# Segment rows and left q and k moved from GpSimd's DMA queue to SyncE's and ScalarE's

## The chip, the cores and the metric

The kernel runs on one core of one Trainium2 chip. Its metric is the time of one execution on the device, in microseconds (us). Before the change the median of three runs is 1866.62 us (1864.03 to 1872.82).

## The reference, cut to what matters

```python
x = A_x                                   # 2048 rows x 1024, bf16
xn = layernorm(x)
return x + A(xn, mem0, Wq, Wk, Wv, Wo, 32) + B(xn, w_r, w_gate, w_up, w_down)

def A(x, mem0, Wq, Wk, Wv, Wo, seg_len):  # 32 heads of 128, 8 memory rows
    mem = mem0
    for s in range(64):                   # segments of 32 rows
        h = concat([mem, x[32 * s:32 * s + 32]])       # 40 rows
        q, k, v = h @ Wq, h @ Wk, h @ Wv               # per head
        o = softmax(mask(q @ k.T * 128 ** -0.5)) @ v @ Wo
        mem = o[:8]                       # the next segment's memory
        outs.append(o[8:])
    return concat(outs)
```

`B` chooses two of the 2048 rows by a router, puts them through a gated MLP of width 3584 and adds the results to those rows. The memory makes the 64 segments a chain: each needs the one before.

## The kernel before, in words

**Rows.** Of a segment's 32 input rows the first 24 go with its 8 memory rows through the loop over segments, 32 rows at a time. The last 8 rows of a segment don't depend on anything but x in q, k and v; these "left" rows are taken for four segments together (a group: 32 left rows), and their q and k are stored to DRAM (`ql_d`) one group ahead. In the code `s` is the segment, `G` its group and `j` its place in the group (0 to 3; I call them first to fourth).

**Weights.** Wq, Wk, Wv and Wo are cut into 64 granules of 512 KB, numbered 0 to 63. 44 stay in SBUF; 20 are streamed from DRAM in each segment (`STREAMED`: 2, 5, 6, 9, 13, 17, 21, 25, 29, 33, 36, 39, 42, 45, 47, 50, 53, 56, 59, 62). From the second segment on granule 6 and half of 25 come from PSUM, so 19 loads a segment remain, `g<-wsc` at line 366, one of them of 256 KB. They go through five buffers ("slots"). "Load 39" is the load of granule 39. `fetch` is called after a granule's use and loads the one four places on; the load waits for TensorE to be done with the slot, which held the granule five places back.

**A segment.** Phases 0 to 5 project q, k and v, two halves each, from eight granules each (line 817); attention runs between them; phase 6 is the projection with Wo (line 586); at the end VectorE adds the result to the rows (line 885), and the 8 memory rows are turned into the next segment's input. `hook(p, kc, fn)` calls `fn` after granule `kc` of phase `p`. Each engine does its instructions in the order in which this program writes them; a queue's instruction that waits holds all behind it.

**Transfers.** SyncE (SP) issues the weight loads. GpSimd issues `load_seg` (four transfers of 24 rows x 256 columns, for the next segment, at hook (2, 4)), the four stores of a segment's output at its end, `new_lx` (left q and k of this segment, from `ql_d`, at granule 9 of phase 6), and the left rows' loads and stores. ScalarE issues the stores to `ql_d` (line 628): of a group's four, one at the start of phase 1 in the second segment, one at the start of phase 2 in the third, and one at the end of phase 5 in each of the two.

**Semaphores.** Each transfer has a completion semaphore. GpSimd's transfers share eight of them (`DMASW0` to `DMASW7`); SP's and ScalarE's share another eight (`DMAHW0` to `DMAHW7`), given out in turn over both engines. A transfer that gets a semaphore waits, on the engine that issues it, until the transfer that had it last has landed.

`X[s % 2]` holds a segment's rows: loaded, then scaled in place (`norm_seg`, line 294), then the sum with the output (`OB`), which is stored from it. A load of segment s + 1 therefore waits for the stores of segment s - 1.

Of the kernel before, what the change touches and what calls it, by code (L numbers as in the profile page):

```python
# [50 lines left out]
def kernel(  # L51
# [16 lines left out]
    nc = tc.nc  # L68
# [4 lines left out]
    SEG = int(A_seg_len)  # L73
# [9 lines left out]
    XM = SEG - M  # L83
# [3 lines left out]
    x2 = A_x[0]  # L87
    out2 = out[0]
# [37 lines left out]
    ql_d = [dram.tile([4, P, 512], BF16, name=f"ql_d{t}") for t in range(NT)]  # L126
# [25 lines left out]
    X = [const.tile([P, 256], BF16, name=f"X{b}") for b in range(2)]  # L152
# [46 lines left out]
    for s in range(4):  # L199
        nc.vector.tensor_copy(out=SELM[:, s, :, 0:XM],  # L200
                              in_=IDENT[:, 32 * s:32 * s + XM].unsqueeze(1).to_broadcast([P, 4, XM]))
        nc.vector.tensor_copy(out=SELL[:, s, :, :],
                              in_=IDENT.rearrange("p (s c) -> p s c", c=32)[:, :, XM:SEG])
        nc.vector.tensor_copy(out=SELR[:, s, :, :],
                              in_=IDENT.rearrange("p (s c) -> p c s", c=32)[:, XM:SEG, :])
# [67 lines left out]
    def two_rows(m, tag):  # L273
        t = one.tile([P, 4], F32, tag=tag, name="RI")
        nc.vector.tensor_copy(out=t[:, 0:1], in_=m[:, 0:1])
        nc.vector.reciprocal(out=t[:, 1:2], in_=m[:, 1:2])
        return t

    def load_seg(s):
        for g in range(4):  # L280
            nc.gpsimd.dma_start(out=X[s % 2][32 * g:32 * g + XM, :],  # L281
                                in_=x2[s * SEG:s * SEG + XM, 256 * g:256 * (g + 1)])

    def norm_seg(s):

        x = X[s % 2]
        mr = two_rows(MR[:, s, :], "ri")
        ab = mr[:, 2:4]
        nc.vector.tensor_scalar(out=ab[:, 0:1], in0=mr[:, 1:2], scalar1=1.0, scalar2=KMSK, op0=ALU.add, op1=ALU.mult)
        nc.vector.tensor_scalar(out=ab[:, 1:2], in0=mr[:, 0:1], scalar1=mr[:, 1:2], scalar2=-1.0, op0=ALU.mult, op1=ALU.mult)  # L290
        xn = front.tile([P, 256], BF16, tag="st", name="XN")
        nc.vector.tensor_scalar(out=xn[:, :], in0=x[:, :], scalar1=mr[:, 0:1], scalar2=mr[:, 1:2],
                                op0=ALU.subtract, op1=ALU.mult)
        nc.vector.tensor_scalar(out=x[:, :], in0=x[:, :], scalar1=ab[:, 0:1], scalar2=ab[:, 1:2],
                                op0=ALU.mult, op1=ALU.add)
        return xn
# [8 lines left out]
    def gview(st):  # L305
        return st.rearrange("p (g c) r -> p c g r", c=2)

    def turn_rows(xn, xl):

        return turn(xn), turn(xl, 1) if xl is not None else None  # L310

    def new_st(turned):
        PTx, PTl = turned
        st = front.tile([P, KC, SEG], BF16, tag="st", name="ST")
        nc.scalar.copy(out=gview(st)[:, :, :, 0:XM], in_=PTx[:, :, :, 0:XM])
        if PTl is None:
            return st, None
        stl = one.tile([P, KC, SEG], BF16, tag="stl", name="STL")
        nc.scalar.copy(out=gview(stl), in_=PTl[:, :, :, :])
        return st, stl  # L320

    def mem_to_st(OB, st):
        PTm = turn(OB)
        nc.vector.tensor_copy(out=gview(st)[:, :, :, XM:SEG], in_=PTm[:, :, :, XM:SEG])
# [11 lines left out]
    def norm_left(t, G):  # L336
        mr = two_rows(MLR[:, G, :], "ri")
        nc.vector.tensor_scalar(out=t[:, :], in0=t[:, :], scalar1=mr[:, 0:1], scalar2=mr[:, 1:2],
                                op0=ALU.subtract, op1=ALU.mult)

    def sum_left(t, G):

        mr = two_rows(ML[:, G, :], "ri")
        nc.vector.tensor_scalar(out=mr[:, 0:1], in0=mr[:, 0:1], scalar1=mr[:, 1:2], scalar2=-1.0,
                                op0=ALU.mult, op1=ALU.mult)
        nc.vector.tensor_scalar(out=mr[:, 1:2], in0=mr[:, 1:2], scalar1=1.0, scalar2=None, op0=ALU.add)
        nc.vector.tensor_scalar(out=t[:, :], in0=t[:, :], scalar1=mr[:, 1:2], scalar2=mr[:, 0:1],
                                op0=ALU.mult, op1=ALU.add)
# [20 lines left out]
    def part(t, jq):  # L369
        return t[jq][:, :] if isinstance(t, list) else t[:, 512 * jq:512 * (jq + 1)]  # L370
# [16 lines left out]
    def bring_back(c, copy):  # L387
        back[c] = one.tile([P, 512], BF16, tag=(roles[0], "bE", "kt", "bC")[c], name="BK")
        copy(out=back[c][:, :], in_=KEPT_COLS[KEPT_WHOLE][c])  # L389

    def kept_piece(g, c, copy):
        t = [t for q, t in queued if q == g][0]
        copy(out=t[:, 512 * c:512 * (c + 1)], in_=KEPT_COLS[g][c])  # L393
# [38 lines left out]
    load_x(0)  # L432
    nc.sync.dma_start(out=WRB, in_=B_w_r.unsqueeze(0).to_broadcast([P, D]))
    load_seg(0)
    XL0 = load_left(0, one.tile([P, 256], BF16, tag="vl0", name="XL0")[:, :])
    OB = one.tile([P, 256], BF16, tag="bA", name="MEM0")
# [21 lines left out]
    norm_left(XL0, 0)  # L458
    ST, STL = new_st(turn_rows(norm_seg(0), XL0))
    mem_to_st(OB, ST)  # L460

# [30 lines left out]
    def new_lx(s):  # L492
        t = lx[0] = one.tile([P, 512], BF16, tag="bA", name="LX")
        G, j = divmod(s, 4)
        nc.gpsimd.dma_start(out=t[:, :], in_=ql_d[G].rearrange("m (x s) c -> (m x) s c", s=4)[:, j])  # L495

    lx = [None]

# [60 lines left out]
        return out  # L559

    after_first = []

    def begin(u):
        PS = psL.tile([P, 512], F32, tag="accl", name="WL" if u == "o" else "PSl")
        units[u] = [PS, 16 if u == "o" else 8]
# [66 lines left out]
    for s in range(NSEG):  # L632
        G, j = divmod(s, 4)
# [9 lines left out]
        def hook(p, kc, fn):  # L643
            hooks.setdefault((p, kc), []).append(fn)
# [128 lines left out]
        def run_passes(p, kc):  # L773

            for u, g in passes.pop((p, kc), []):
                if g == 8 * p + kc or p >= 7:
                    t = res_tiles[g] if p >= 7 else held[g]
                else:
                    t = held.get(g) or res_tiles[g]
                one_pass(u, g, t)  # L780
# [7 lines left out]
            hook(2, 3, lambda: sum_left(xl_of[0], G - 1))  # L788
        hook(*((1, 0) if s > 0 else (2, 3)), clear_pl)
        if s > 0:  # L790
            hook(0, 0, lambda: bring_back(3, nc.scalar.copy))
            hook(0, 1, lambda: bring_back(0, nc.vector.tensor_copy))
            hook(2, 1, lambda: kept_piece(KEPT_PART, 2, nc.vector.tensor_copy))
            hook(2, 2, lambda: kept_piece(KEPT_PART, 3, nc.vector.tensor_copy))
# [1 line left out]
        hook(3, 4, exponent)  # L796
        hook(3, 4, lambda: soften(0))
        if s + 1 < NSEG:
            hook(2, 4, lambda: load_seg(s + 1))
        if j == 0 and G + 1 < NT:  # L800
            hook(4 if s == 0 else 1, 1, get_left)
            hook(5, 3, lambda: norm_left(nxt["xl"], G + 1))
# [6 lines left out]
        for p, (mat, half) in enumerate(PHASES):  # L809
# [3 lines left out]
            for kc in range(KC):  # L813
                g = 8 * p + kc
                Gv = back if s > 0 and g == KEPT_WHOLE else granule(g)
                for jq in range(4):
                    nc.tensor.matmul(PSm[32 * jq:32 * jq + 32, :], lhsT=ST[:, kc, :], rhs=part(Gv, jq),  # L817
                                     start=(kc == 0), stop=(kc == KC - 1), tile_position=(0, 32 * jq))
# [45 lines left out]
        for w in range(16):  # L864
            if w == 5:
                attend(1, 0)
            if w == 8 and s + 1 < NSEG:
                attend(1, 1, lambda: turned.append(turn_rows(xn, left_too)))
                nxt["st"], stl = new_st(turned[0])
                STL = stl or STL  # L870
            elif w == 8:
                attend(1, 1)
            Gv = granule(48 + w)
            project(WO, w, Gv, lhs_main, w == 15, first=(w == 0))
            held[48 + w] = Gv
            run_passes(6, w)
            if w == 9 and s + 1 < NSEG:
                new_lx(s + 1)
                bring_back(1, nc.scalar.copy)
                bring_back(2, nc.vector.tensor_copy)  # L880
            if w == 11 and j == 3:
                xl_of[0] = load_left(G, one.tile([P, 256], BF16, tag="stl", name="OL")[:, :], True)
            release(6, w)
        OB = X[s % 2]
        nc.vector.tensor_tensor(out=OB[:, :], in0=WO[:, 0:256], in1=OB[:, :], op=ALU.add)  # L885
        for g in range(4):
            nc.gpsimd.dma_start(out=out2[s * SEG:s * SEG + XM, 256 * g:256 * (g + 1)], in_=OB[32 * g:32 * g + XM, :])  # L887
        run_passes(7, 0)
        if s + 1 < NSEG:
            mem_to_st(OB, nxt["st"])  # L890
# [1 line left out]
        assert not passes and not held, (passes, held.keys())  # L892
        if s + 1 < NSEG:
            ST = nxt["st"]
    sum_left(xl_of[0], NT - 1)
    copy_unit("o", NSEG - 1, "vector")

# [53 lines left out]
    rows = [nc.sync.value_load(I8[0:1, c:c + 1], min_val=0, max_val=S - 1) for c in range(2)]  # L951
# [62 lines left out]
```

## Time and profile before

| | |
|---|---|
| median of three runs | 1866.62 us (1864.03 to 1872.82) |
| the profiled execution | 1871.21 us |
| its span, first to last instruction | 1869.1 us |
| mean granted TensorE clock | 0.957 of full speed |
| TensorE matmul busy | 1568.8 us (84%) |
| VectorE, ScalarE, GpSimd busy | 896.9 (48%), 683.6 (37%), 457.1 us (24%) |
| moved by DMA | 712.27 MB, mean 381 GB/s |

The profile names engines PE (TensorE matmul), PEld (its weight load), DVE (VectorE), ACT (ScalarE), POOL (GpSimd) and SP (SyncE); a q behind the name (SPq, ACTq) means its sequencer, which waits and issues. L366 is line 366 of the kernel. A row such as `out<-in` names tiles by the program's names without numbers. A row of waits gives the waiting engine and line, who ended the wait, the total in us, how many, and the longest. "DMA to landing" is the time from a transfer's issue to its semaphore.

### The profile page before, as it was taken

The page shows a single profiled execution, that of the slowest core. Times are in us where ns is not written, and L with a number is a line of the kernel's source. Part 1 is how long each engine was busy: PE and PEld are TensorE (multiplying, and loading weights), DVE is VectorE, ACT ScalarE, POOL GpSimd, SP SyncE. Part 2 cuts the span into 40 slices and gives each one's busy share as a digit, 9 for nine tenths or more (in the row PEclk, how much of TensorE's full clock was granted, in tenths as well). Part 3 has the DMA queues.
Part 4 walks back from the last instruction along what each step waited for, and adds up shares of the span by engine and source line. Part 5 has one row for each costly group of instructions (what it writes and reads, how often), then busy time and mean ns, then how long its engine had stood idle before and what let it go on. Part 6 is the DMA issues. An engine that isn't in the chain of part 4 may idle for free.

```text
span 1869.1 us, 80529 instructions
## 1 busy us (share of the span) xinstructions
PE 1568.8 (84%) x34978; PEld 847.9 (45%) x34978; DVE 896.9 (48%) x2950; ACT 683.6 (37%) x1933; POOL 457.1 (24%) x898
## 2 busy tenths in 40 slices
PE   3458998898998988888899988988889988988764
PEld 1124444444444444444444444444445544444433
DVE  6725544554455444544554455544544455445430
ACT  1113433444343433434344334434334343433320
POOL 3111322213231322223132322323132221312220
PEclk8669999999999999999999999999999999999995
DMA  9999999999999999999999999999999999999998
GB/s 370 406 355 373 388 386 380 393 382 387 394 385 392 366 383 391 359 380 385 388 375 388 389 384 387 373 396 374 378 369 396 394 382 383 378 377 352 384 402 338
DMA packets 230322, 712.27 MB, mean 381 GB/s; under 512 B 39040, under 2 KB 52912, under 8 KB 229968
## 3 DMA queue, kind: packets, MB, share of 16 engines
q1 hardware_dynamic: 192592, 671.18, 93.0%
q0 software_dynamic: 28736, 28.08, 4.7%
q10 hardware_dynamic: 8640, 7.87, 1.2%
q8 instruction: 274, 4.49, 0.9%
q14 instruction: 80, 0.66, 0.1%
HBM read 694.32 MB, written 22.29 MB: 383 GB/s over the span
## 4 chain that ended last, share of the span: by engine, by line
DMA 61%; PE 32%; DVE 4%; issue 1%; ACT 1%; SPq 0%; ACTq 0%; DVEq 0%
DMA g<-wsc 54%; PE PSm L817 17%; PE WO L586 4%; PE PSl L579 4%; PE BT L649 2%; DMA XP<-in_A_x_dram 2%; PE WL L598 1%; DMA MW<-in_B_w_gate_dram 1%; DVE XR L256 1%; DMA MW<-in_B_w_up_dram 1%; DMA g<-in_A_Wq_dram 1%; DMA wres<-in_A_Wo_dram 1%; DMA g<-in_A_Wo_dram 1%; DMA MW<-in_B_w_down_dram 1%; DMA g<-in_B_w_down_dram 1%
## 5 line engine op out<-in xcount | busy, mean ns | idle before, releaser
L817 PE MATMUL PSm<-wres,ST 128*32 128x512 bf16 x8448 | 700.5, 383 | 6.5 <-DMA wres<-in_A_Wv_dram 3.5
L817 PEld LDWEIGHTS <-ST 128*32 128x32 bf16 x12288 | 323.6, 96 | 412.7 <-issue 168.2
L817 PE MATMUL PSm<-g,ST 128*32 128x512 bf16 x3588 | 360.0, 386 | 97.7 <-DMA g<-wsc 76.3
L586 PEld LDWEIGHTS <-OT 128*32 128x32 bf16 x8192 | 217.6, 97 | 166.6 <-issue 141.0
L836 ACT CAST XB<-PSm 128x512 bf16<-128x512 f32 x256 | 150.7, 589 | 283.9 <-PE PSm L817 280.8
L586 PE MATMUL WO<-wres,OT 128*32 128x256 bf16 x5632 | 237.6, 278 | 12.3 <-DMA wres<-in_A_Wo_dram 8.0
L495 POOL DMA_DIRECT2D LX<-ql_d x63 | 35.4, 562 | 814.0 <-PE WO L586 423.2
L586 PE MATMUL WO<-g,OT 128*32 128x256 bf16 x2560 | 133.3, 281 | 84.1 <-DMA g<-wsc 72.6
L579 PE MATMUL PSl<-wres,STL 128*32 128x512 bf16 x2112 | 184.5, 390 | 0.4 <-issue 0.4
L887 POOL DMA_DIRECT2D out_dram<-X x256 | 130.2, 515 | 211.9 <-DVE X L885 169.4
L664 DVE COPY KT<-BT 128x512 bf16<-128x512 bf16 x112 | 45.9, 410 | 278.7 <-issue 121.8
L281 POOL DMA_DIRECT2D X<-in_A_x_dram x256 | 130.1, 515 | 179.6 <-PE PSm L817 88.8
L389 ACT COPY BK<-KEPT 128x512 bf16<-128x512 bf16 x126 | 74.3, 590 | 131.2 <-PE WO L586 99.8
L657 ACT COPY QT<-BT 128x512 bf16<-128x512 bf16 x128 | 75.0, 586 | 127.1 <-PE BT L502 78.1
L649 PEld LDWEIGHTS <-XB 128*128 128x128 bf16 x1024 | 58.6, 98 | 117.1 <-ACT XB L836 75.2
L885 DVE TENSOR_TENSOR X<-WO,X 128x256 bf16<-128x256 f32 x64 | 27.2, 425 | 172.3 <-PE WO L586 172.3
L649 PE MATMUL BT<-IDENT,XB 128*128 128x128 bf16 x1024 | 102.2, 223 | 8.2 <-ACT XB L836 6.7
L579 PEld LDWEIGHTS <-STL 128*32 128x32 bf16 x3072 | 84.0, 98 | 53.0 <-issue 8.5
L846 ACT CAST VM<-PSm 128x512 bf16<-128x512 f32 x128 | 76.5, 598 | 83.3 <-PE PSm L817 82.8
L736 PEld LDWEIGHTS <-VM 32*128 32x128 bf16 x2048 | 65.1, 91 | 83.7 <-issue 72.7
L393 DVE COPY g<-KEPT 128x512 bf16<-128x512 bf16 x126 | 47.6, 420 | 101.7 <-PE PSm L817 51.5
L681 DVE TENSOR_TENSOR BS<-BS,CT 128x96 f32<-128x96 f32 (+1 forms) x256 | 59.1, 231 | 72.8 <-PE BS L674 68.3
(175 smaller groups left out, 2371.9 us busy)
## 6 DMA issues: line engine op xcount, KB each, us to landing
g<-wsc SPq DMA_DIRECT2D x1134, 512.0 KB, 6.0
g<-wsc SPq DMA_DIRECT2D x63, 256.0 KB, 5.7
LX<-ql_d POOLq DMA_DIRECT2D x63, 128.0 KB, 5.6
ql_d<-XBl ACTq DMA_DIRECT2D x60, 128.0 KB, 5.8
MW<-in_B_w_gate_dram SPq DMA_DIRECT2D x16, 448.0 KB, 9.5
MW<-in_B_w_up_dram SPq DMA_DIRECT2D x16, 448.0 KB, 9.1
wres<-in_A_Wk_dram SPq DMA_DIRECT2D x12, 512.0 KB, 11.9
MW<-in_B_w_down_dram SPq DMA_DIRECT2D x12, 512.0 KB, 10.1
```

Of the source, the lines that this page charges most:

```text
L281: nc.gpsimd.dma_start(out=X[s % 2][32 * g:32 * g + XM, :], in_=x2[s * SEG:s * SEG + XM, 256 * g:256 * (g + 1)])
L389: copy(out=back[c][:, :], in_=KEPT_COLS[KEPT_WHOLE][c])
L579: nc.tensor.matmul(PSl[32 * jq:32 * jq + 32, :], lhsT=STL[:, g % KC, :], rhs=part(Gv, jq), start=first_, stop=last_, tile_position=(0, 32 ...
L586: nc.tensor.matmul(PS[32 * g:32 * g + 32, 0:256], lhsT=lhs(h), rhs=Gv[:, D * hs + 256 * g:D * hs + 256 * (g + 1)], start=(first and hs == ...
L649: nc.tensor.transpose(out=PTq[:, il, :, :].rearrange("p j r -> p (j r)"), in_=XB[:, il * P:(il + 1) * P], identity=IDENT[:, :])
L657: nc.scalar.copy(out=QT[half][:, :, :], in_=pv)
L681: nc.vector.tensor_tensor(out=S4, in0=S4, in1=m, op=ALU.add)
L736: nc.tensor.matmul(o, lhsT=VM[half][q0:q0 + 32, il * P:(il + 1) * P], rhs=PTm[q0:q0 + 32, il, 0:NK], start=True, stop=False, tile_position ...
L817: nc.tensor.matmul(PSm[32 * jq:32 * jq + 32, :], lhsT=ST[:, kc, :], rhs=part(Gv, jq), start=(kc == 0), stop=(kc == KC - 1), tile_position= ...
L836: nc.scalar.copy(out=XB[:, :], in_=PSm[:, :])
L846: nc.scalar.copy(out=VM[half][:, :], in_=PSm[:, :])
L887: nc.gpsimd.dma_start(out=out2[s * SEG:s * SEG + XM, 256 * g:256 * (g + 1)], in_=OB[32 * g:32 * g + XM, :])
```

## The change

Three kinds of transfer change their queue, and two also their place:

- the stores of a segment's output rows go from GpSimd at the segment's end to SP, at hook (0, 3) of the next segment (behind the last segment for the last one), still 24 rows each;
- the loads of the next segment's rows go from GpSimd at hook (2, 4) to SP at hook (3, 0), and take all 32 rows (the 8 more are masked: their scale is 0);
- the load of left q and k goes from GpSimd to ScalarE at the same place.

GpSimd keeps the left rows' loads and stores. The diff:

```diff
--- before.py
+++ after.py
@@ -278,8 +278,8 @@
 
     def load_seg(s):
         for g in range(4):
-            nc.gpsimd.dma_start(out=X[s % 2][32 * g:32 * g + XM, :],
-                                in_=x2[s * SEG:s * SEG + XM, 256 * g:256 * (g + 1)])
+            nc.sync.dma_start(out=X[s % 2][32 * g:32 * (g + 1), :],
+                              in_=x2[s * SEG:(s + 1) * SEG, 256 * g:256 * (g + 1)])
 
     def norm_seg(s):
 
@@ -492,7 +492,7 @@
     def new_lx(s):
         t = lx[0] = one.tile([P, 512], BF16, tag="bA", name="LX")
         G, j = divmod(s, 4)
-        nc.gpsimd.dma_start(out=t[:, :], in_=ql_d[G].rearrange("m (x s) c -> (m x) s c", s=4)[:, j])
+        nc.scalar.dma_start(out=t[:, :], in_=ql_d[G].rearrange("m (x s) c -> (m x) s c", s=4)[:, j])
 
     lx = [None]
 
@@ -559,6 +559,12 @@
         return out
 
     after_first = []
+    done = []
+
+    def store_rows():
+        t, rows = done.pop()
+        for g in range(4):
+            nc.sync.dma_start(out=out2[t * SEG:t * SEG + XM, 256 * g:256 * (g + 1)], in_=rows[32 * g:32 * g + XM, :])
 
     def begin(u):
         PS = psL.tile([P, 512], F32, tag="accl", name="WL" if u == "o" else "PSl")
@@ -788,6 +794,7 @@
             hook(2, 3, lambda: sum_left(xl_of[0], G - 1))
         hook(*((1, 0) if s > 0 else (2, 3)), clear_pl)
         if s > 0:
+            hook(0, 3, store_rows)
             hook(0, 0, lambda: bring_back(3, nc.scalar.copy))
             hook(0, 1, lambda: bring_back(0, nc.vector.tensor_copy))
             hook(2, 1, lambda: kept_piece(KEPT_PART, 2, nc.vector.tensor_copy))
@@ -796,7 +803,7 @@
         hook(3, 4, exponent)
         hook(3, 4, lambda: soften(0))
         if s + 1 < NSEG:
-            hook(2, 4, lambda: load_seg(s + 1))
+            hook(3, 0, lambda: load_seg(s + 1))
         if j == 0 and G + 1 < NT:
             hook(4 if s == 0 else 1, 1, get_left)
             hook(5, 3, lambda: norm_left(nxt["xl"], G + 1))
@@ -883,8 +890,7 @@
             release(6, w)
         OB = X[s % 2]
         nc.vector.tensor_tensor(out=OB[:, :], in0=WO[:, 0:256], in1=OB[:, :], op=ALU.add)
-        for g in range(4):
-            nc.gpsimd.dma_start(out=out2[s * SEG:s * SEG + XM, 256 * g:256 * (g + 1)], in_=OB[32 * g:32 * g + XM, :])
+        done.append((s, OB))
         run_passes(7, 0)
         if s + 1 < NSEG:
             mem_to_st(OB, nxt["st"])
@@ -892,6 +898,7 @@
         assert not passes and not held, (passes, held.keys())
         if s + 1 < NSEG:
             ST = nxt["st"]
+    store_rows()
     sum_left(xl_of[0], NT - 1)
     copy_unit("o", NSEG - 1, "vector")
```

What it does to the order is seen in the third segment of a group (s = 26). SP before, from load 21 to load 53; behind each row stand the semaphores that it waits for (PE_49 and DVE_49 are those of TensorE and VectorE):

```order
L366 DMA g_19008<-wsc21_110 128x2048 [waits DMAHW6_49,DMAHW3_49,PE_49]
L366 DMA g_19034<-wsc25_111 128x1024 [waits DMAHW7_49,PE_49]
L366 DMA g_19068<-wsc29_112 128x2048 [waits DMAHW0_49,PE_49]
L366 DMA g_19096<-wsc33_113 128x2048 [waits DMAHW1_49,PE_49]
L366 DMA g_19127<-wsc36_114 128x2048 [waits DMAHW2_49,PE_49]
L366 DMA g_19191<-wsc39_115 128x2048 [waits DMAHW3_49,PE_49]
L366 DMA g_19228<-wsc42_116 128x2048 [waits DMAHW4_49,DVE_49,PE_49]
L366 DMA g_19253<-wsc45_117 128x2048 [waits DMAHW5_49,PE_49]
L366 DMA g_19278<-wsc47_118 128x2048 [waits DMAHW7_49,PE_49]
L366 DMA g_19334<-wsc50_119 128x2048 [waits DMAHW0_49,PE_49]
L366 DMA g_19364<-wsc53_120 128x2048 [waits DMAHW6_49,DMAHW1_49,PE_49]
```

And now, from load 21 to load 39 (L281 are the segment loads; a row's first DMAHW is mostly the semaphore that it gets itself):

```order
L366 DMA g_19008<-wsc21_110 128x2048 [waits DMAHW1_49,PE_49]
L366 DMA g_19034<-wsc25_111 128x1024 [waits DMAHW3_49,PE_49]
L366 DMA g_19068<-wsc29_112 128x2048 [waits DMAHW4_49,DMAHW2_49,PE_49]
L366 DMA g_19096<-wsc33_113 128x2048 [waits DMAHW5_49,PE_49]
L366 DMA g_19123<-wsc36_114 128x2048 [waits DMAHW6_49,PE_49]
L281 DMA X1_131<-in_A_x_dram 32x256 [waits DMAHW7_49]
L281 DMA X1_131<-in_A_x_dram 32x256 [waits DMAHW0_49]
L281 DMA X1_131<-in_A_x_dram 32x256 [waits DMAHW1_49]
L281 DMA X1_131<-in_A_x_dram 32x256 [waits DMAHW2_49]
L366 DMA g_19191<-wsc39_115 128x2048 [waits DMAHW3_49,PE_49]
```

The segment loads stand between loads 36 and 39, and load 39 behind the fourth of them. Between load 21 (DMAHW1) and load 25 (DMAHW3) the turn skips DMAHW2. ScalarE in the same segment shows who has it; before (L628):

```order
L836 CAST XB_19082<-PSm_19020 128x512 [waits PE_49]
L627 CAST XBl_19089<-PSl_18953 128x512 [waits DMAHW3_49,DMAHW7_49,DVE_49,PE_49]
L628 DMA ql_d7_96<-XBl_19089 128x512 [waits DMAHW6_49,Activation_49]
L662 COPY KT_19112<-QKL_19054 128x16x8 [waits PE_49]
L836 CAST XB_19175<-PSm_19084 128x512 [waits PE_49]
```

and now (L634, the same line moved):

```order
L843 CAST XB_19082<-PSm_19020 128x512 [waits PE_49]
L633 CAST XBl_19089<-PSl_18949 128x512 [waits DMAHW0_49,DMAHW3_49,DVE_49,PE_49]
L634 DMA ql_d7_96<-XBl_19089 128x512 [waits DMAHW2_49,Activation_49]
L668 COPY KT_19112<-QKL_19054 128x16x8 [waits PE_49]
L843 CAST XB_19171<-PSm_19084 128x512 [waits PE_49]
```

Its store to `ql_d` has DMAHW2, which the fourth segment load then waits for. Before it had DMAHW6, and the next to wait for that was load 53, the last row of the first list.

The second segment of a group (s = 25), SP before, loads 21 to 39:

```order
L366 DMA g_18322<-wsc21_110 128x2048 [waits DMAHW1_49,PE_49]
L366 DMA g_18351<-wsc25_111 128x1024 [waits DMAHW2_49,PE_49]
L366 DMA g_18381<-wsc29_112 128x2048 [waits DMAHW3_49,PE_49]
L366 DMA g_18407<-wsc33_113 128x2048 [waits DMAHW4_49,PE_49]
L366 DMA g_18442<-wsc36_114 128x2048 [waits DMAHW5_49,PE_49]
L366 DMA g_18501<-wsc39_115 128x2048 [waits DMAHW6_49,PE_49]
```

and now, loads 21 to 39:

```order
L366 DMA g_18322<-wsc21_110 128x2048 [waits DMAHW4_49,PE_49]
L366 DMA g_18351<-wsc25_111 128x1024 [waits DMAHW5_49,PE_49]
L366 DMA g_18381<-wsc29_112 128x2048 [waits DMAHW6_49,PE_49]
L366 DMA g_18407<-wsc33_113 128x2048 [waits DMAHW7_49,PE_49]
L366 DMA g_18438<-wsc36_114 128x2048 [waits DMAHW0_49,PE_49]
L281 DMA X0_130<-in_A_x_dram 32x256 [waits DMAHW1_49]
L281 DMA X0_130<-in_A_x_dram 32x256 [waits DMAHW2_49]
L281 DMA X0_130<-in_A_x_dram 32x256 [waits DMAHW3_49]
L281 DMA X0_130<-in_A_x_dram 32x256 [waits DMAHW4_49]
L366 DMA g_18501<-wsc39_115 128x2048 [waits DMAHW5_49,PE_49]
```

with ScalarE now:

```order
L389 COPY BK_18284<-KEPT1_194 128x512 [waits DVE_49,PE_49,Activation_49]
L843 CAST XB_18336<-PSm_18279 128x512 [waits PE_49,Activation_49]
L633 CAST XBl_18343<-PSl_18255 128x512 [waits DMASW6_49,DMASW5_49,DMASW7_49,DMASW0_49,DVE_49]
L634 DMA ql_d7_96<-XBl_18343 128x512 [waits DMAHW0_49,Activation_49]
L663 COPY QT_18369<-BT_134 128x512 [waits PE_49]
```

Here ScalarE's store has DMAHW0, and load 36 waits for it; the four segment loads stand behind load 36.

## The prediction

> **What bounds the kernel now.** I read the page first: queues, then the chain that ended last.
>
> ```profile
> PE 1568.8 (84%) x34978; PEld 847.9 (45%) x34978; DVE 896.9 (48%) x2950; ACT 683.6 (37%) x1933; POOL 457.1 (24%) x898
> DMA packets 230322, 712.27 MB, mean 381 GB/s; under 512 B 39040, under 2 KB 52912, under 8 KB 229968
> q1 hardware_dynamic: 192592, 671.18, 93.0%
> q0 software_dynamic: 28736, 28.08, 4.7%
> q10 hardware_dynamic: 8640, 7.87, 1.2%
> DMA 61%; PE 32%; DVE 4%; issue 1%; ACT 1%; SPq 0%; ACTq 0%; DVEq 0%
> ```
>
> q1 is SP's queue, q0 GpSimd's, q10 ScalarE's. The sixteen DMA engines count as taken almost all the time, 93% of it by SP's weight stream, and 61% of the chain is DMA. Next the waits, TensorE's and SP's own:
>
> ```profile
> PE PSm L817 <- DMA g<-wsc: 76.3, 154, 2.5
> PE WO L586 <- DMA g<-wsc: 72.6, 150, 2.0
> SPq L366 <- PE PSm L817: 422.9, 640, 2.7
> SPq L366 <- DMA g<-wsc: 396.5, 740, 2.5
> SPq L366 <- PE PSl L579: 213.6, 239, 3.0
> ```
>
> TensorE waits 149 us for granules. SP waits over 1033 us, for TensorE to free one of the five slots or for the slot's last load. So it is a ring: a granule is used, SP issues the load into its slot, the load lands some 6 us later. Such a ring is hurt by whatever holds SP back for longer than the loads in flight last. Where that is, three stretches of one segment show (the third of its group of four, 798.13 to 825.08 us; the last two columns are DMA share and GB/s):
>
> ```profile
> 798.13:803.50 5.37, 4.22 (x72) 1.93 (x69) 1.28 (x5) 0.80 (x2) 2.26 (x5) 1.00 1.01 403
> 803.50:808.90 5.40, 5.40 (x122) 2.67 (x118) 1.72 (x6) 3.03 (x6) 2.01 (x4) 1.00 0.88 260
> 808.90:825.08 16.18, 13.87 (x353) 8.03 (x350) 9.83 (x32) 6.51 (x22) 0.55 (x1) 1.00 1.02 404
> ```
>
> For 5.4 us in the middle TensorE is busy all the time and the transfers fall to 260 GB/s: there the ring has drained and has room. Around it they run at 403 and 404 and TensorE has gaps: there a load that comes late is paid for. These durations are of the profiled execution, 1871.2 us; the median of the runs is 1866.6, so I form differences against the former and add them to the latter.
>
> **The change part by part.** First the transfers as work. Per segment four stores, four loads and one left q and k load leave GpSimd's queue. By the rows of the issues:
>
> ```profile
> LX<-ql_d POOLq DMA_DIRECT2D x63, 128.0 KB, 5.6
> ql_d<-XBl ACTq DMA_DIRECT2D x60, 128.0 KB, 5.8
> X<-in_A_x_dram POOLq DMA_DIRECT2D x256, 12.0 KB, 5.2
> out_dram<-X POOLq DMA_DIRECT2D x256, 12.0 KB, 5.1
> ```
>
> That is 63 x 131 KB + 512 x 12.3 KB = 14.5 MB before; the wider segment loads (32 rows for 24) make it 15.6 MB. At q0's price (28.08 MB in 4.7%) the old bytes take 2.4% of the engines' time. The new ones take 2.4% at the price of q10, whose rows are small like these (7.87 MB in 1.2%), 2.2% at q1's and 2.6% at q0's. So I take 0, between -5 and +3 us.
>
> Instructions: SP issues eight more per segment. No row shows SP issuing such a transfer; the nearest are its granule loads, 0.32 us, and two four-row stores at 0.62 (min/median/max in ns; the second row tells the granule loads' time to landing in us). For ScalarE its ql_d stores are the nearest, and the last two rows are GpSimd's (busy us, mean ns, idle before):
>
> ```profile
> L366 SPq DMA_DIRECT2D g<-wsc x1197: 319/320/1167, 119.1 to 1802.1; - x200
> DMA to landing us min/median/max: 3.3/6.0/10.3
> L978 SPq DMA_DIRECT2D out_dram<-T x2: 533/618/702, 1864.4 to 1866.2; - x2
> L628 ACTq DMA_DIRECT2D ql_d<-XBl x60: 325/327/361, 136.9 to 1669.2; - x60
> L495 POOL DMA_DIRECT2D LX<-ql_d x63 | 35.4, 562 | 814.0 <-PE WO L586 423.2
> L887 POOL DMA_DIRECT2D out_dram<-X x256 | 130.2, 515 | 211.9 <-DVE X L885 169.4
> ```
>
> 8 x 0.32 to 0.62 us is 2.6 to 5.0 us in a segment of 26.9. SP waits for more than half of the span, and each batch of four takes about 1.5 us, with three or more loads in flight: 0 for the issuing itself. ScalarE gets one issue a segment, 0.33 us, and is busy 37% of the span: 0. GpSimd loses nine issues of about 0.52 us; it is busy 24% of the span and idle before them for want of what TensorE and VectorE make, so it sets no end: 0.
>
> Now the waits. SP's and ScalarE's transfers share eight completion semaphores, taken in turn, and each waits for the landing of the transfer that had its semaphore eight transfers ago. Before, the segment's load stream met only itself there, and eight back was long landed. With nine more transfers in the turn, SP waits in three new places.
>
> (a) The last two stores, behind which load 21 stands, wait for LX or for load 2 to land; loads 21 to 33 and 39 to 47 wait for the landing of the granule four back, where a freed slot five back was enough. Three loads are in flight meanwhile, 1.6 MB or 4 us at 404 GB/s. I take 0; the bounds are 0 and 0.3 us a segment (18 us in all) if they run dry a little.
>
> (b) In the third segment of each group, the fourth segment load waits for the ql_d store that ScalarE issued in this same segment, and load 39 and all later ones stand behind it on SP. In the segment above (ScalarE's cast and store, the time of that store to landing, SP's issue of load 39, TensorE's use of granule 39):
>
> ```profile
> 805.51 0.59 ACT L627 CAST XBl<-PSl 128x512 bf16<-128x512 f32 x1
> 806.13 0.33 ACTq L628 DMA_DIRECT2D ql_d<-XBl  x1
> DMA to landing us min/median/max: 6.3/6.3/6.3
> 806.97 0.32 SPq L366 DMA_DIRECT2D g<-wsc  x1
> 813.38 0.40 PE L817 MATMUL PSm<-g,ST 128*32 128x512 bf16 x4
> ```
>
> Load 39 went out at 806.97 and TensorE used it at 813.38. With the change SP sits until the store has landed, 806.13 + 6.3 = 812.43; the segment load and its issue take 0.4, so load 39 goes out at 812.85. By the fastest landing of the run, 3.3 us, it is there at 816.15: 2.8 us late. By the usual 6.0 it would be 5.5 us late. I take 2.8, since by 812.85 the queue is empty and the fastest landing is the nearest row. Little is won back: the stretch behind runs at 404 GB/s with the engines full. If half of it came back all the same, 1.4 us would stay, so the bounds are 1.4 and 5.5. There are 60 such stores, four to a group, thus 15 such segments: 15 x 2.8 = 42 us (21 to 82).
>
> (c) In the second segment of each group load 36 waits likewise (ScalarE's store and its landing, the issue of load 36 and its landing, the issue of load 39 and its landing, in the segment that begins at 770.8):
>
> ```profile
> 775.27 0.33 ACTq L628 DMA_DIRECT2D ql_d<-XBl  x1
> DMA to landing us min/median/max: 5.2/5.2/5.2
> 778.36 0.32 SPq L366 DMA_DIRECT2D g<-wsc  x1
> DMA to landing us min/median/max: 5.6/5.6/5.6
> 779.89 0.32 SPq L366 DMA_DIRECT2D g<-wsc  x1
> DMA to landing us min/median/max: 5.2/5.2/5.2
> ```
>
> The store lands at 780.5, so load 36 goes out 2.2 us after its 778.36 and lands at 783.8 by the fastest landing, against 778.36 + 5.6 = 784.0 before: not late. The four segment loads behind it take 1.5 us of SP, so load 39 goes out at 782.4 instead of 779.89 and lands at 785.7. Before, it was there at 785.1. That is 0.6 us late, and 3.3 if it takes 6.0. I take 0.7 with the row that follows, near the lower end for the same reason as in (b): 15 x 0.7 = 10 us (0 to 50).
>
> At the end of the second and third segments load 13 waits for the group's late ql_d stores, about 1 us, with three loads in flight: 0. SP's first four loads and last four stores lie among transfers that keep SP's queue full: 0.
>
> Sum: 0 + 0 + 42 + 10 = +52 us, 1923 against the profiled execution and 1919 against the median.
>
> **Where the Trainium skill would put it.** By "DMA: Bandwidth & Descriptors", section "Issuing engines are not separate DMA queues", all queues end in the same sixteen engines, and moving transfers between issuing engines saves or costs only the sequencer's time, usually small. By that rule the sum would be the transfers' work alone, no change, 1867 us. The rows above agree that the work is the same on either queue (2.4% and 2.4%); the rule leaves out what an in-order issuer waits for.
>
> **The rivals.** *No change:* the new waits are met in time. For it: in the stretch of 260 GB/s transfers have room, and a wait that ended there would cost nothing. Against: the held load is used at 813.38, in the stretch without room, and the store lands 5.4 us after load 39 used to go out. It decides 3.3 + 0.4 us before the use, at 809.7: the store would have to land in 3.6 us, and this one takes 6.3. Time: 1862 to 1870, say 1867.
>
> *Faster (the other side):* GpSimd's queue slows the others, and with its 14.5 MB at q1's price 0.28% of 1871 us, 5 us, comes back, more if packets of two queues cost each other time. For it: q0 moves 6.0 MB for a percent and q1 7.2. Against: q10, a hardware queue with small rows, moves 6.6, hardly more than q0. It decides only if SP's waits cost under 5 us. Time: 1855 to 1861.
>
> *Much slower:* the held loads land in their usual 6.0 us, because ScalarE's and SP's transfers queue up together when the hold ends. Then (b) is 82, (c) 50 and with (a) 18: up to 2017, typically 1985. For it: 6.0 us is the median of all landings. Against: four granules at 404 GB/s take 5.2 us, so most of those 6.0 is queueing behind loads that are gone after the hold.
>
> **How the numbers follow.** Slower by the sums of (b) and (c): 0.78, its own range 1893 to 1950 (21 + 5 above the median, and 60 + 24 for terms that are both over the middle). Much slower: 0.12. No change: 0.06. Faster: 0.04. Half a percent, 9 us, is about what this measurement can tell from no change. The predicted time is 1919. The range 1885 to 1965 leaves out the two fast cases (0.10) and most of the much slower one. Slower by over 0.5%: 0.90; within: 0.06; faster: 0.04.
>
> **What the new profile would show.** Right: SP's own waits have a new row for DMA ql_d, 15 times and some 5 us each, at the segment loads; load 36 has one of about 2 us; TensorE waits for g<-wsc longer by about 50 us in all, in second and third segments alone; third segments are about 2.8 us longer, first and fourth ones unchanged; LX lands within 6 us from ScalarE. q1 and q10 grow by what q0 loses. Wrong: if first and fourth segments lengthen as much, (a) is the cause; if the ql_d wait on SP is there but third segments keep their length, the ring has more room than I found; if there is no such row, the turn of the semaphores isn't what holds SP.

## The result, and the profile after

The kernel became slower: 2048.9 us (median; 2031.7 to 2069.8) against 1865.3 for the kernel before in the same runs, a ratio of 1.096 (95% interval 1.092 to 1.099). I had forecast 1919, in a range of 1885 to 1965. Ratios, here and below, leave out slow executions, such as the one of 2069.8 us here and one of 7721 us in the run with LX alone. The profiled execution took 2048.3 us, its span 2046.7.

From the page of the kernel after: engines, transfers, queues, and the chain that ended last.

```profile
PE 1614.0 (79%) x34978; PEld 864.1 (42%) x34978; DVE 904.0 (44%) x2950; ACT 690.5 (34%) x1933; POOL 159.0 (8%) x323
DMA packets 241490, 713.29 MB, mean 349 GB/s; under 512 B 35968, under 2 KB 66096, under 8 KB 241136
q1 hardware_dynamic: 214096, 678.55, 88.9%
q10 hardware_dynamic: 17712, 16.13, 2.3%
q0 software_dynamic: 9328, 13.47, 1.9%
DMA 70%; PE 24%; DVE 2%; SPq 1%; issue 1%; ACT 1%; ACTq 0%; DVEq 0%
```

The bytes are the same to 1 MB, but they move at 349 GB/s instead of 381, and DMA is now 70% of the chain. The work of the three queues together, 93.1% of 2046.7 us, is 1905 us of the engines' time; before it was 98.9% of 1869.1, 1849 us. So the packets also took 57 us longer in all, which the runs don't explain. With the 0.9 and 1.0% of two small queues that the page also lists, the engines now stand free for 6% of the span, and before for next to nothing: loads are not issued in time. The waits, TensorE's first, then SP's own (total us, times, longest):

```profile
PE PSm L824 <- DMA g<-wsc: 212.7, 293, 3.3
PE WO L592 <- DMA g<-wsc: 75.5, 134, 1.9
SPq L366 <- DMA g<-wsc: 394.2, 563, 2.8
SPq L366 <- PE PSm L824: 155.2, 294, 2.5
SPq L567 <- DMA LX<-ql_d: 145.4, 60, 5.7
SPq L366 <- PE PSl L585: 87.0, 118, 2.6
SPq L366 <- DMA ql_d<-XBl: 73.1, 33, 3.7
SPq L281 <- DMA ql_d<-XBl: 70.8, 16, 6.7
```

TensorE waits 288 us for granules where it waited 149. That is 139 of the 178 us by which the span grew; 45 more are TensorE's busy time, at a mean granted clock of 0.942 against 0.957 (the ratio of the clocks accounts for 25 of them; the other 20 I can't place), and its other gaps shrank by some 6. On SP, waiting for TensorE has shrunk (line 817, now 824: 422.9 to 155.2 us), and waiting for transfers has taken its place: the two foreseen rows with ql_d (144 us together), and one that I had costed at nothing, the stores at line 567 behind LX (145 us, nearly every segment). SP's row of waits for granules is no longer than before (396.5 to 394.2 us).

Most of it shows in the third segment that the prediction used (s = 26, now 863.41 to 894.72 us). Stretches first (the last two columns are DMA share and GB/s), then SP's issues in order and ScalarE's store:

```profile
863.41:868.80 5.39, 4.89 (x82) 2.32 (x85) 1.29 (x5) 1.08 (x3) 0.00 (x0) 1.00 0.83 297
868.80:874.20 5.40, 5.32 (x120) 2.65 (x116) 2.14 (x6) 3.15 (x7) 0.00 (x0) 1.00 0.94 329
874.20:894.72 20.52, 13.51 (x346) 8.08 (x345) 9.48 (x31) 6.11 (x22) 0.24 (x1) 1.00 0.88 332
```

```profile
863.72 0.80 SPq L366 DMA_DIRECT2D g<-wsc  x2
864.56 3.34 SPq L567 DMA_DIRECT2D out_dram<-X  x4
868.01 3.04 SPq L366 DMA_DIRECT2D g<-wsc  x5
871.10 6.66 SPq L281 DMA_DIRECT2D X<-in_A_x_dram  x4
877.86 3.59 SPq L366 DMA_DIRECT2D g<-wsc  x5
```

```profile
870.78 0.33 ACTq L634 DMA_DIRECT2D ql_d<-XBl  x1
```

The stretch at the start ran at 403 GB/s and the last one at 404; now they run at 297 and 332. Load 21 goes out 4.6 us after the segment's start; before it was 1.6. Load 13 has waited for a ql_d store until 0.25 us after the start, and behind load 17 the four stores take 3.3 us: only 0.7 of that is the wait for LX (2.4 us in the mean of all segments), and 1.45 us is the issue of the fourth store alone. The four segment loads take 6.7 us, because the fourth waits for the ql_d store of 870.78, and load 39 goes out 14.45 us after the start, where it went out at 8.84.

How long segments are is read from the ends of VectorE's addition (line 885, now 892), as means over segments 4 to 62:

| | first | second | third | fourth |
|---|---|---|---|---|
| before, us | 27.2 | 26.5 | 26.7 | 26.2 |
| after | 28.3 | 29.7 | 31.1 | 28.6 |
| longer by | 1.2 | 3.2 | 4.3 | 2.4 |

Third segments grew most, but first and fourth ones, which I had forecast unchanged, grew too: a quarter and over half as much as the third. The prediction had said that if they lengthened as much as third ones, (a) would be the cause. By that sign (a) has a part in it, and isn't all.

### The profile page after: what moved, and what is told of

Read it like the earlier page. It is cut to its first block, busy times and chain, and to the rows that moved or that the text cites. A ratio compares the mean times of both kernels' runs of the same rounds, so it can differ in the third digit from the quotient of the medians.

```text
span 2046.7 us, 80321 instructions
## 1 busy us (share of the span) xinstructions
PE 1614.0 (79%) x34978; PEld 864.1 (42%) x34978; DVE 904.0 (44%) x2950; ACT 690.5 (34%) x1933; POOL 159.0 (8%) x323
## 4 chain that ended last, share of the span: by engine, by line
DMA 70%; PE 24%; DVE 2%; SPq 1%; issue 1%; ACT 1%; ACTq 0%; DVEq 0%
DMA g<-wsc 59%; PE PSm L824 11%; PE WO L592 4%; PE PSl L585 3%; DMA ql_d<-XBl 3%; DMA LX<-ql_d 2%; DMA XP<-in_A_x_dram 1%; PE BT L655 1%; PE WL L604 1%; DMA MW<-in_B_w_down_dram 1%; DVE XR L256 1%; DMA MW<-in_B_w_up_dram 1%; DMA g<-in_A_Wq_dram 1%; DMA MW<-in_B_w_gate_dram 1%; DMA wres<-in_A_Wo_dram 1%
## 5 line engine op out<-in xcount | busy, mean ns | idle before, releaser
L824 PE MATMUL PSm<-wres,ST 128*32 128x512 bf16 x8448 | 713.2, 389 | 6.4 <-DMA wres<-in_A_Wv_dram 3.0
L824 PEld LDWEIGHTS <-ST 128*32 128x32 bf16 x12288 | 332.7, 97 | 589.1 <-issue 355.8
L824 PE MATMUL PSm<-g,ST 128*32 128x512 bf16 x3588 | 367.8, 395 | 238.9 <-DMA g<-wsc 212.7
L592 PE MATMUL WO<-wres,OT 128*32 128x256 bf16 x5632 | 241.8, 283 | 12.7 <-DMA wres<-in_A_Wo_dram 7.8
L585 PE MATMUL PSl<-wres,STL 128*32 128x512 bf16 x2112 | 192.0, 402 | 1.4 <-issue 1.2
L702 DVE TENSOR_REDUCE DN<-BS 128x8 f32<-128x320 f32 x128 | 62.9, 492 | 97.8 <-ACT BS L697 97.3
L892 DVE TENSOR_TENSOR X<-WO,X 128x256 bf16<-128x256 f32 x64 | 27.2, 425 | 174.6 <-PE WO L592 174.6
L751 DVE CAST OT<-BT 128x128 bf16<-128x128 f32 x128 | 37.3, 292 | 148.9 <-PE BT L744 76.5
L585 PE MATMUL PSl<-g,STL 128*32 128x512 bf16 x900 | 92.7, 393 | 0.0
L742 PE MATMUL BT<-PT,VM 32*128 32x40 bf16 x1024 | 88.5, 179 | 1.0 <-issue 0.9
```

The costliest lines, as they stand in the source:

```text
L585: nc.tensor.matmul(PSl[32 * jq:32 * jq + 32, :], lhsT=STL[:, g % KC, :], rhs=part(Gv, jq), start=first_, stop=last_, tile_position=(0, 32 ...
L592: nc.tensor.matmul(PS[32 * g:32 * g + 32, 0:256], lhsT=lhs(h), rhs=Gv[:, D * hs + 256 * g:D * hs + 256 * (g + 1)], start=(first and hs == ...
L702: nc.vector.tensor_reduce(out=DN[:, :], in_=S8, axis=AX.X, op=ALU.add)
L742: nc.tensor.matmul(o, lhsT=VM[half][q0:q0 + 32, il * P:(il + 1) * P], rhs=PTm[q0:q0 + 32, il, 0:NK], start=True, stop=False, tile_position ...
```

## The experiments

Three theories went into them. Theory 1: the stores' wait for LX. Theory 2: the turn of eight semaphores itself, in which eight small transfers a segment make each granule load wait for the landing of the granule four back. Theory 3: small rows on SP's queue are slow as such. The kernel before, run beside them in three groups, took 1866.2, 1866.1 and 1865.5 us.

### Taking ScalarE's transfers out of the turn

**LX back on GpSimd**, against the kernel after:

```diff
-        nc.scalar.dma_start(out=t[:, :], in_=ql_d[G].rearrange(...)[:, j])
+        nc.gpsimd.dma_start(out=t[:, :], in_=ql_d[G].rearrange(...)[:, j])
```

> The change with the load of left q and k (LX) back on GpSimd's queue; stores and segment loads stay on SyncE. Theory 1 (the segment's output stores, which stand ahead of load 21 on SyncE, wait for LX to land; 145 us of SyncE's waits are that): the 126 us by which first to fourth segments grew beyond the 40 or so that the ql_d waits explain come back, so 1925 us (1905 to 1955), and load 21 goes out at about 2 us after the segment's start instead of 2.6 to 5. Theory 2 (the turn: with eight more transfers in it each granule load waits for the landing of the granule four back, and four granules in flight are too few): the LX wait is only replaced by one for a granule, 2010 to 2045 us. Theory 3 (small-row transfers slow SyncE's queue as such): 2020 to 2050 us.

Measured 2029.1 us, 1.091 (1.086 to 1.096) of before. **ql_d stores on GpSimd**, against the kernel after:

```diff
-            stores.append(lambda: nc.scalar.dma_start(out=ql_d[Gu]...
+            stores.append(lambda: nc.gpsimd.dma_start(out=ql_d[Gu]...
```

> The change with the stores to ql_d on GpSimd's queue; LX stays on ScalarE, stores and segment loads on SyncE. All three theories: the waits for ql_d at the segment loads and at load 36 are gone, and second and third segments come down to the length of first ones, 28.4 us, so about 60 us come back: 1985 us (1970 to 2005). If third segments keep more than 30 us, the ql_d wait was not what lengthened them; if the time falls below 1930, the ql_d waits also cost in the segments behind them.

Measured 1986.9 us, 1.067 (1.063 to 1.071), as all three theories had it. **Both edits together:**

> The change with both LX and the ql_d stores on GpSimd's queue, so that SyncE's transfers share their semaphores with nobody: what is left of the change are the stores and segment loads on SyncE. Theory 1: 1870 to 1890 us (at most the 18 us that the prediction gave the turn). Theory 2: still slow in every segment, 1930 to 1980 us, with load 39 waiting for load 25's landing and load 25 for load 9's. Theory 3: 1930 to 1980 us too, with SyncE's issues long (0.4 to 1.7 us) and fewer GB/s around them.

Measured 1947.3 us, 1.046 (1.041 to 1.051). SP's rows, in this order (two of the first run, two of the second, one of the third):

```profile
SPq L366 <- DMA g<-wsc: 551.1, 673, 3.1
...
SPq L281 <- DMA ql_d<-XBl: 66.7, 16, 5.3
```

```profile
SPq L366 <- DMA g<-wsc: 470.5, 672, 3.1
...
SPq L567 <- DMA LX<-ql_d: 132.0, 62, 3.6
```

```profile
SPq L366 <- DMA g<-wsc: 604.1, 792, 3.3
```

Theory 1 falls: it had put the first run at 1905 to 1955 us and the third at 1870 to 1890. Without LX in the turn SP's 145 us of waiting for it are gone, but its waiting for granules rises from 394 to 551 us, and only 20 us come back. Each wait taken away uncovers the next. The four kernels give a table: the ql_d stores cost 62 us with LX in the turn (2048.9 - 1986.9) and 82 without (2029.1 - 1947.3); LX costs 20 or 40; and 81 us stay when SP shares its semaphores with nobody. Those 81 are stores and segment loads alone.

**LX on ScalarE alone**, in the kernel before:

> The kernel before with nothing but LX moved to ScalarE. It is awaited by load 29 or 33, which goes out 4 to 5 us after the segment's start, when LX has landed (2.2 us after it). Theories 1 to 3: no change, 1860 to 1875 us. If LX on ScalarE's queue is slow as such, it is slower here too: over 1885 us.

Measured 1864.9 us, 1.000 (0.997 to 1.003). SP waits for LX in this run too, 13 times:

```profile
SPq L366 <- DMA LX<-ql_d: 13.1, 13, 3.4
```

So LX on ScalarE's queue costs nothing by itself, though SP also waits 36.4 us for ql_d stores here (22 times; before 0.3 us). LX costs where the eight new turns have brought the wait for it forward, from load 29 or 33 to the stores ahead of load 21.

### Turns or rows

**Turns without rows.** The kernel before, the ql_d stores on GpSimd, and SP issues this at hooks (0, 3) and (3, 0):

```diff
+    def four_turns(n):
+        for k in range(4):
+            nc.sync.dma_start(out=pad_d[4 * n + k:4 * n + k + 1, :], in_=IDENT[0:1, :])
```

> The kernel before (ql_d stores on GpSimd, so that nobody else shares SyncE's semaphores), and SyncE issues eight transfers of 256 bytes more per segment, into DRAM that nobody reads, at the two places where the change puts its stores and segment loads: the turns without the rows. Theory 2 (each granule load behind them waits for the granule four back; four in flight are too few): 1930 to 1955 us, as the change without its ScalarE transfers (1947). Theory 3 (small rows on SyncE's queue take the stream's time): 1860 to 1875 us. In between, a share to each.

Measured 1936.3 us, 1.036 (1.031 to 1.041), within theory 2's range: 70 of the 81 us, with 0.2 MB more than before moved in all. **Rows without turns.** The third run above, with one transfer for four:

```diff
-        for g in range(4):
-            nc.sync.dma_start(out=X[s % 2][32 * g:32 * (g + 1), :],
-                              in_=x2[s * SEG:(s + 1) * SEG, 256 * g:256 * (g + 1)])
+        nc.sync.dma_start(out=X[s % 2][:, :], in_=x2[s * SEG:(s + 1) * SEG, :].rearrange("r (g c) -> g r c", g=4))
...
-        for g in range(4):
-            nc.sync.dma_start(out=out2[t * SEG:t * SEG + XM, 256 * g:256 * (g + 1)], in_=rows[32 * g:32 * g + XM, :])
+        nc.sync.dma_start(out=out2[t * SEG:(t + 1) * SEG, :].rearrange("r (g c) -> g r c", g=4), in_=rows[:, :])
```

> The change with LX and the ql_d stores on GpSimd, and the four stores of a segment as one transfer, the four loads as one: the same rows of 512 bytes, at the same places on SyncE, in two turns instead of eight (the store takes 32 rows a segment instead of 24; the left rows' store comes behind it). Theory 2: six turns less, so granules five back again nearly everywhere: 1870 to 1890 us. Theory 3: the rows are the same, 1935 to 1960 us. If SyncE's own eight issues of 0.4 us were the cost, about a quarter of the 81 us stays, 1885.

Measured 1901.6 us, 1.020 (1.015 to 1.024), 12 us above the upper end of theory 2. What was left is not in the segments: their means are 27.4, 26.4, 26.4 and 26.1 us, the old ones, and the last one ends at 1807.0 us against 1810.8 before. It is in the tail behind it, 82 us instead of 58. GpSimd's own wait there:

```profile
POOL out_dram L627 <- DMA out_dram<-X: 46.6, 1, 46.6
```

The left rows' store now comes behind the 32-row store, SP's last store stood behind the MLP's weights, and GpSimd's loads for the MLP stood behind its own store. **The last segment stored by GpSimd, as before the change:**

```diff
+        if s + 1 == NSEG:
+            done.pop()
+            for g in range(4):
+                nc.gpsimd.dma_start(out=out2[s * SEG:s * SEG + XM, 256 * g:256 * (g + 1)], in_=OB[32 * g:32 * g + XM, :])
...
-    store_rows()
     sum_left(xl_of[0], NT - 1)
```

> As the run with one store and one load transfer a segment, but the last segment's output is stored by GpSimd as before the change: in that run the segments had their old length (the last one ended at 1807.0 us against 1810.8), and GpSimd's last store of left rows waited 46.6 us for SyncE's last store, which lay behind the MLP's weights. Theory 2: 1855 to 1868 us, the kernel before or a few us less. If it stays at 1885 or above, the tail is not the cause of what was left, and small rows on SyncE's queue cost about 20 us after all.

Measured 1874.0 us, 1.004 (1.001 to 1.007). The tail was the cause. The time stays 6 us above what theory 2 gave; it is not a version that beats the kernel before.

**Stores alone** and **loads alone**, each moved to SP in the kernel before:

> The kernel before with nothing but the output stores moved to SyncE, at the change's place. Theory 2: four turns in a segment, loads 21 to 33 and 39 to 47 wait for the granule four back: 1890 to 1930 us (half of the 81 us, and load 36 waits for ql_d in second segments). Theory 3: 3.1 MB of small rows on SyncE, about half of 81 us too: this run alone doesn't tell the two apart, it tells what the stores are worth.

Measured 1932.6 us, 1.036 (1.030 to 1.041): 3 us above the expected range, and 66 above the kernel before.

> The kernel before with nothing but the segment loads moved to SyncE (32 rows, at the change's place). Theory 2: loads 39 to 47 wait for the granule four back, 1890 to 1930 us, and where a segment load waits for ql_d in second segments these lengthen by 1 to 3 us more. Theory 3: likewise about half of the 81 us. Tells what the loads are worth; with the stores alone, whether the two add up.

Measured 1948.6 us, 1.045 (1.040 to 1.049): 19 us above the expected range, and 82 above the kernel before. As announced, these two price the parts and don't tell theories 2 and 3 apart. They include the waits for ql_d, which stays on ScalarE in both, so they are not halves of the 81.

### How many turns

The run with the turns alone, with **three** transfers at each place and with **five** (`range(3)`, `range(5)`):

> As the run with the turns alone, with three transfers of 256 bytes at each of the two places instead of four. Theory 2: the load behind three turns waits for the granule five back, whose slot it needs free anyway, so nothing is added: 1860 to 1875 us. Theory 3 in its last form (each small transfer on SyncE costs a share by itself, eight cost 70): six cost 53 us, 1910 to 1925 us.

Measured 1874.5 us, 1.003 (1.000 to 1.006).

> The same with five transfers of 256 bytes at each place. Theory 2: six loads a segment wait for the granule three back, so three in flight at most, and the stream runs well below its 390 GB/s behind each place: 1990 to 2080 us. Theory 3 in its last form: ten cost 88 us, 1945 to 1965 us.

Measured 2086.8 us, 1.119 (1.113 to 1.125): 7 us above theory 2's range, and 122 above that of theory 3. Three rows of each run, of three, four and five turns: all transfers, SP's waits at the loads for a granule to land, and TensorE's. (With five turns SP waits another 42.5 us for granules at the small transfers themselves.)

```profile
DMA packets 225321, 712.39 MB, mean 381 GB/s; under 512 B 39796, under 2 KB 45988, under 8 KB 224964
SPq L367 <- DMA g<-wsc: 348.1, 669, 2.3
PE PSm L824 <- DMA g<-wsc: 71.8, 144, 2.1
```

```profile
DMA packets 225574, 712.43 MB, mean 367 GB/s; under 512 B 40048, under 2 KB 46240, under 8 KB 225216
SPq L367 <- DMA g<-wsc: 712.6, 864, 3.7
PE PSm L824 <- DMA g<-wsc: 145.1, 232, 2.8
```

```profile
DMA packets 225827, 712.47 MB, mean 344 GB/s; under 512 B 40300, under 2 KB 46492, under 8 KB 225468
SPq L367 <- DMA g<-wsc: 761.5, 792, 3.5
PE PSm L824 <- DMA g<-wsc: 240.4, 337, 3.0
```

Six small transfers a segment cost 9 us (0 to 12 by the interval), eight 70, ten 221. A price per transfer would go up evenly; this has a step where theory 2 puts it. Eight semaphores less three are a wait for the granule five back, which the slot asks for anyway. Less four, only four granules can be in flight; less five, three. The traces bear this out. Right after the issue of each of the loads 21 to 29 and 39 to 45, in segments 8 to 59, there are 4.3 to 5.0 granules in flight in the mean before and with three turns, never more than four with four turns, and never more than three with five. The bytes that landed between 6 and 8 us after a segment's start, averaged over segments 8 to 59, show the same: 359 GB/s before, 364 with three turns, 318 with four, 261 with five.

### ScalarE's transfers without the turns

The run with one transfer each and the last store on GpSimd, **with LX and the ql_d stores on ScalarE** as in the change:

> The change with one store and one load transfer a segment (last segment's store on GpSimd), and LX and the ql_d stores on ScalarE as in the change. Theory 2: the ql_d stores are now waited for by load 42 in second and load 50 in third segments, which go out about when they have landed, and LX by load 21 in second segments and by load 25 in third and fourth, which lose 0 to 2 us each: 1865 to 1900 us. If ScalarE's transfers in the turn cost by themselves, what they cost beside eight more turns (2049 less 1947, 102 us) stays: over 1930 us.

Measured 1887.5 us, 1.011 (1.006 to 1.017). SP still waits for both:

```profile
SPq L364 <- DMA LX<-ql_d: 77.5, 53, 4.0
SPq L364 <- DMA ql_d<-XBl: 54.2, 46, 2.7
```

132 us of such waits cost 14 us beside two turns (1887.5 - 1874.0; the waits are those of the profiled execution, the fastest of four at 1874.7). Beside eight they cost 102 (2048.9 - 1947.3), with 289 us of waits. So a tenth of their length comes through in the one case and a third in the other. I take this as the effect of the fuller ring: with five granules in flight SP may sit for a while, with four less so. But the waits also fall at other loads in the two kernels, and no run separates the two.

## Why the prediction was wrong

**Transfers' work 0, issuing 0: about right.** One transfer for four, the rows nearly unchanged, is 1.004 (1.001 to 1.007) of before, 8 us with the two turns that are left; the bounds were -5 and +3. Of the 81 us that stores and loads cost, 70 come with turns of 256 bytes; the 11 between (1947.3 and 1936.3) are what rows and longer issues may cost beside the turns.

**(a), taken as 0 and bounded by 18 us: the step that failed.** It named the mechanism exactly, "loads 21 to 33 and 39 to 47 wait for the landing of the granule four back", and dismissed it with "three loads are in flight meanwhile, 1.6 MB or 4 us". The turns alone cost 70 us, 1.1 us in a segment. The wait for LX, the other half of (a), cost 20 to 40 more. The rows at hand would have warned of it: with a landing of 6.0 us, five granules of 524 KB in flight allow 437 GB/s, four 350, three 262 (an estimate). The stream ran at 381 in the mean and at 404 where TensorE waits, so by this five suffice and four don't. The estimate is a rough one, since it holds the landing at 6.0: in the traces load 29, with 5.0, 4.0 and 3.0 granules in flight, takes 5.6 us to land before, 5.0 with four turns and 4.8 with five. The test was whether the ring stays full, not whether something is in flight.

**(b) and (c), 52 us (bounds 21 to 132): right mechanism, sized somewhat low.** Taking the ql_d stores out of the turn gives 62 or 82 us. SP waits 16 times for 70.8 us at the segment loads (foreseen: 15 times, some 5 us each), and load 39 goes out 5.6 us later (foreseen: 5.9). In third segments load 39 then lands in 3.8 us in the mean, near the 3.3 that I took for (b); in second ones it takes 5.7, where I had gone by 3.3 too, so (c) was too small. What I had taken as 0 beside them, load 13 at the ends of second and third segments, is most of the row of 33 waits and 73.1 us, 2.2 us each in the mean: all but four lie there. Load 36, my (c), waits for ql_d in those four alone. In the other second segments the store has landed when load 36's turn comes, because in the mean it lands 2.4 us earlier in the segment than before and load 36 comes 1.5 us later.

**LX lands within 6 us from ScalarE:** mostly not. For the segment above it was issued at 860.25, and the stores that wait for it went on at 866.1, 5.9 us later; but over all 63 the median is 6.3 us (5.1 to 8.0).

```profile
860.25 0.33 ACTq L495 DMA_DIRECT2D LX<-ql_d  x1
```

**The rivals.** "Much slower" came nearer, with at most 2017 us, but for another reason: it made (b) and (c) dearer, and left (a) at its 18. "No change" and "faster" fail. By the Trainium skill, "DMA: Bandwidth & Descriptors", section "Issuing engines are not separate DMA queues", issuing transfers from several engines at once saves only the sequencer's time. The runs agree for the transfers as work (1.004 with two turns, 1.000 for LX alone). They show what that rule doesn't speak of: nearly the same bytes from another issuer cost 183 us, since their place in the issuer's order and in its shared semaphores changes too.

**The sum, by runs:** stores and loads 81 (70 of them turns), the ql_d stores 62 to 82, LX 20 to 40; 183 in all, as 81 + 82 + 20 or 81 + 62 + 40 (these are differences along two ways from one kernel to the other, so they must add up). Open stays the part of TensorE's lower clock and of the 57 us of longer packets, which no run isolates.

## What to carry to other kernels

Where transfers share a fixed set of completion semaphores in turn, a small transfer takes as much of the turn as a large one: count how many of the big ones can still be in flight at each place, and price that as (granules in flight x size) / landing time against the rate that the stream needs. As the landing gets shorter when fewer are in flight, take that as a warning and measure. A wait on an issuing queue cost a tenth of its length here beside two turns and a third beside eight, so the parts of such a change must not be priced one by one. If a transfer must move to the streaming queue, make it one transfer instead of four, and look at what its last one stands behind.

## What was unexpected of the hardware

Where small transfers stand among the granule loads, single issues on SP get long, those of granules too. The rows of stores, segment loads and granules in the kernel after (min/median/max in ns) reach 1.7 us:

```profile
L567 SPq DMA_DIRECT2D out_dram<-X x256: 302/357/1718, 130.8 to 2030.7; - x128
L281 SPq DMA_DIRECT2D X<-in_A_x_dram x256: 310/430/1740, 1.9 to 1936.6; - x128
L366 SPq DMA_DIRECT2D g<-wsc x1197: 319/320/1746, 121.3 to 1976.6; - x200
```

Before, the longest issue of a granule was 1.17 us. The medians, 0.36, 0.43 and 0.32 us, are near those of other issues, so this is a matter of a few instructions: 57 of these last over 1 us, and 4 of the granules' before. No run measured its price. TensorE's mean granted clock was lower in most of the kernels that take long (0.942 after, 0.938 with five turns) than in the others (0.957 before, 0.958 with three turns), though not in step with the time: the stores alone ran at 0.959 in 1932.0 us and the loads alone at 0.945 in 1939.9.
